# Sketched attention and a squared-ReLU MLP on one core: loads without holds, half of v on SyncE's queue, one output transfer a chunk, and a new order of work

## The chip, the core and the metric

The kernel runs on one core of a Trainium2 chip. A core has TensorE (PE, matrix products into PSUM), VectorE (DVE), ScalarE (ACT), GpSimd (POOL) and SyncE (SP), which run their own instruction streams and wait for one another through semaphores. Sixteen DMA engines move data between HBM and the core's SBUF; SyncE, ACT and GpSimd can each issue transfers, and each has its own queue on them. In the profile q1 is SyncE's queue, q10 ACT's and q0 GpSimd's. The metric is the device time of one execution in microseconds, as the median of several runs.

## The reference

q, k and v have the shape 4 batches x 4 heads x 1088 positions x 32, and S1 and S2 are 8 x 32 sketches. Each row x of q and k is mapped to 64 features, the products of the 8 numbers S1 x with the 8 numbers S2 x. Attention is then linear:

```python
q_p, k_p = (phi(q), phi(k))                 # phi: outer product of S1 x and S2 x
kv = np.einsum('bhsf,bhsd->bhfd', k_p, v)
z = np.sum(k_p, axis=2)
num = np.einsum('bhsf,bhfd->bhsd', q_p, kv)
den = np.einsum('bhsf,bhf->bhs', q_p, z)[..., None] + 1e-06
attn = num / den
x = attn.transpose(0, 2, 1, 3).reshape(B * S, H * D)      # 4352 x 128
h = x @ w_in                                # w_in 128 x 2048
r = np.maximum(h, 0.0)
out = (r * r) @ w_out                       # w_out 2048 x 128
```

## The kernel before

The four batches of attention are computed one after another, and their output columns are gathered in nine chunks for the MLP: chunks 0 and 1 come from batch 0, 2 and 3 from batch 1, and so on to 7, each of 512 tokens, and chunk 8, of 256 tokens, takes the last two positions of every group of 34 from all four batches. A chunk's MLP has 8 steps u, each over 256 of the 2048 hidden units.

The work is written as a list of small operations (ORDER, L33 to L66), and the list is emitted in that order. All of them are pinned, so each engine executes its share in the order of the list and no other. A name such as `R.1.4@A` is operation R of chunk 1, step 4, on ACT; `@V` is DVE, `@M` is one DVE instruction over two steps. The operations are:

- `kT`, `qT` (L242, L383): DVE transposes k or q of a batch. `ka` (L264): PE multiplies k with the sketches; `kc` (L284): ACT copies that out of PSUM; `kp` (L295): DVE forms the 64 features.
- `kg`, `gs`, `wz`, `wc` (L308 to L337): the sum z over the features, taken as a small product of the sketched k with itself, is multiplied with S2bd on PE (`wz`, L320) and written into the weights Wq by DVE (`wc`, L331). Wq is the right operand of `qa` (L404), so q is sketched and prepared for the denominator in one product.
- `qc` (L431) copies that out; `dt`, `dr`, `da` (L445 to L475) compute the reciprocal of the denominator and scale; `qf` and `qp` (L477, L490) form q's features and transpose them.
- `kv` (L339) multiplies k's features with v on PE, `kt`, `kr`, `kx` (L355 to L380) bring the result into the layout KV. `nd` (L508) multiplies q's features with KV, and `xe` (L537) writes the attention output as x for the MLP.
- `M` (L553) is x times w_in, `R` (L572) the ReLU, `S` (L583) the square, `O` (L593) the product with w_out, `E` (L610) copies a finished chunk to SBUF and issues its output transfers. `W` (L201) is a matmul on zeros into an idle PSUM bank.

PSUM has three pools: ps_h, two tiles of two banks for `M`; ps_o, one bank for `O`; ps_m, three banks for everything of attention. An operation that needs a tile waits until the former user of that buffer has been read.

The loads are not pinned; they are issued early, in the order of their queues. On SyncE's queue are k of batch 0, v of head 0 of batch 0, q of batch 0, and all other k and q. ACT's queue has S1 and S2 (L118, L119), v of head 1 of batch 0 (L154) and four copies of S2 into the block-diagonal S2bd (L184). GpSimd's queue has the rest of batch 0's v, w_in, w_out and v of the other batches; it also casts w_in and w_out to bf16 as they move. A k or q load moves 544 KB, one head's v 128 KB, a remainder of v (the last two positions, L139) 16 KB. The two `hold` operations (L147) copy one element on GpSimd into the k tile of batch 1 and of batch 2 out of a tile that another load fills; the load of that k tile has to come behind the copy. As the queues came out, SyncE issues k0, v0, q0, q1, q2, k3, q3, and then the held k1 and k2.

The number of semaphores for transfers is limited: eight are shared in turn by the transfers of SyncE and ACT, and eight by those of GpSimd, so an issue waits until the transfer that used its semaphore last has landed.

Of the kernel before, what the change touches and what calls it, by code (L numbers as in the profile page):

```python
# [10 lines left out]
F32 = mybir.dt.float32  # L11
# [22 lines left out]
kT.0.0 ka.0.0 kT.0.1 ka.0.1 kc.0.0 kp.0.0 kc.0.1 W.2 kg.0 gs.0 qT.0 W.1 wz.0 wc.0 W.1 qa.0.0  # L34
qc.0.0@A kv.0.0 kp.0.1 kv.0.1 kt.0 dt.0.0 dr.0.0 qa.0.1 kr.0 da.0.0 qf.0.0 qp.0.0 qc.0.1@A
dt.0.1 dr.0.1 kx.0@A W.5 nd.0.0 xe.0.0@A W.1 nd.0.1 xe.0.1@A kT.1.0 ka.1.0 kc.1.0 M.0.0 R.0.0@A
ka.1.1 kc.1.1 M.0.1 M.0.2 R.0.1@A da.0.1 R.0.2@A qf.0.1 qp.0.1 nd.1.0 xe.1.0@A kg.1 gs.1 M.0.3
qT.1 S.0.0@V S.0.1@V O.0.0 R.0.3@A M.0.4 R.0.4@A kp.1.1 wz.1 wc.1 nd.1.1 kT.2.0 M.0.5 O.0.1
M.0.6 xe.1.1@A R.0.5@A qa.1.0 S.0.4@A qa.1.1 qc.1.0@A qc.1.1@A ka.2.0 ka.2.1 kp.1.0 M.1.0
S.0.3@M O.0.2 O.0.3 R.0.6@A kc.2.1 M.1.1 kv.1.0 kv.1.1 R.1.0@A kc.2.0 kg.2 M.1.2 qT.2 R.1.1@A  # L40
kt.1 dt.1.0 gs.2 kr.1 S.0.5@A dr.1.0 M.0.7 R.1.2@A R.0.7@A S.0.6@V wz.2 kx.1@A O.0.4 O.0.5 M.1.3
R.1.3@A kT.3.0 ka.3.0 da.1.0 qf.1.0 kc.3.0 wc.2 qp.1.0 qa.2.0 qa.2.1 qf.1.1 ka.3.1 qc.2.0@A
qc.2.1@A S.0.7@V M.1.4 M.1.5 S.1.2@A kc.3.1 R.1.4@A R.1.5@A O.0.6 O.0.7 qp.1.1 nd.2.0 xe.2.0@A
M.1.6 M.1.7 kp.3.0 S.1.1@M dt.2.0 R.1.6@A kg.3 gs.3 dr.2.0 R.1.7@A nd.3.0 E.0@V da.2.0 M.2.0
xe.3.0@A M.2.1 S.1.3@V R.2.0@A O.1.0 O.1.1 S.1.5@M M.2.2 kp.2.0 O.1.2 R.2.1@A qT.3 R.2.2@A M.2.3
R.2.3@A O.1.3 O.1.4 wz.3 M.2.4 M.2.5 O.1.5 S.1.7@M R.2.4@A R.2.5@A O.1.6 O.1.7 E.1@A S.2.0@A
S.2.3@M wc.3 M.3.0 M.3.1 kp.2.1 S.2.5@M qa.4.0 qc.4.0@A R.3.0@A R.3.1@A qf.2.0 qp.2.0 qa.3.0
qa.3.1 S.2.1@A kv.2.0 kv.2.1 kt.2 M.2.6 M.2.7 R.2.6@A dt.4.0 O.2.0 O.2.1 O.2.2 O.2.3 M.3.2
qf.2.1 qp.2.1 O.2.4 R.2.7@A qc.3.0@A qc.3.1@A M.3.3 S.2.7@M kr.2 R.3.2@A R.3.3@A M.3.4 S.3.0@V
O.2.5 S.3.1@V M.3.5 O.2.6 O.2.7 R.3.4@A R.3.5@A M.3.6 M.3.7 S.3.3@M E.2@A kx.2@V nd.4.0 dt.3.0  # L50
R.3.6@A S.3.6@A xe.4.0@A kp.3.1 kv.3.0 kv.3.1 kt.3 S.3.5@M R.3.7@A nd.5.0 xe.5.0@A O.3.0 dr.3.0
da.3.0 M.4.0 M.4.1 dr.4.0 R.4.0@A qf.3.0 qf.3.1 qp.3.0 qp.3.1 O.3.1 O.3.2 R.4.1@A S.3.7@V O.3.3
M.4.2 M.4.3 R.4.2@A S.4.2@V R.4.3@A O.3.4 O.3.5 M.4.4 R.4.4@A kr.3 kx.3@V M.4.5 R.4.5@A O.3.6
O.3.7 M.5.0 M.5.1 E.3@A S.4.0@V nd.6.0 R.5.0@V S.4.1@V S.4.3@V S.5.0@V R.5.1@A M.5.2 xe.6.0@A
M.4.6 O.4.0 O.4.1 S.4.5@M R.5.2@A R.4.6@A M.4.7 R.4.7@A O.4.2 O.4.3 M.5.3 R.5.3@A M.5.4 O.4.4
R.5.4@A O.4.5 da.4.0 M.5.5 S.5.1@V qf.4.0 qp.4.0 nd.8.0 R.5.5@A S.4.7@M M.6.0 xe.8.0@A O.4.6
S.5.3@M S.5.4@V M.6.1 R.6.0@A O.4.7 M.5.6 E.4@A R.6.1@V nd.7.0 M.5.7 R.5.6@A R.5.7@A M.6.2
# [612 lines left out]
```

## Time and profile before

| | |
|---|---|
| median of 3 runs | 124.7 us (124.58 to 125.56) |
| profiled execution | 124.32 us, its span 122.5 us |
| busy PE, DVE, ACT, GpSimd | 104.1, 96.8, 86.4, 17.1 us |
| mean granted TensorE clock | 0.944 |
| moved by DMA | 10.25 MB; read 8.79 MB, written 2.23 MB |
| q1 (SyncE), q0 (GpSimd), q10 (ACT) | 6.75, 3.04, 0.20 MB |

The span begins with the first instruction and ends with the last. PE's busy share counts the time from a matmul's start to its modelled end. In the slices of the page a digit is the busy share of an engine in tenths in a 40th of the span, 3.06 us. The chain of waits follows the work that ended last back from the end, and names what each step waited for. A wait belongs to the instruction that stood at the head of its engine's queue; all that is behind it waits as well.

### The profile page before, as it was taken

To read this page: it belongs to the slowest core of one execution; us is meant where nothing else is said; L and a number is where in the kernel's file an instruction comes from. 1 tells how busy PE (TensorE), PEld (TensorE's weight loads), DVE (VectorE), ACT (ScalarE), POOL (GpSimd) and SP (SyncE) were. 2 spreads that over 40 slices of the span, in tenths; PEclk is the share of its full clock that TensorE was granted. 3 is DMA by queue.
4 is the path that set the end of the run, shared out by engine and by line. 5 is a ranking of instruction groups with operands and counts; after the bars stand their busy time and mean duration, and the time that the engine had idled before them with its cause. 6 is when DMAs were issued, how large, how long until landed. Compare 5 with 4: busy or idle time off the path is not lost.

```text
span 122.5 us, 4127 instructions
## 1 busy us (share of the span) xinstructions
PE 104.1 (85%) x1807; PEld 75.1 (61%) x1807; DVE 96.8 (79%) x153; ACT 86.4 (71%) x138; POOL 17.1 (14%) x32
## 2 busy tenths in 40 slices
PE   6094009993999999999999999999999999999950
PEld 1063007942577888756777865676666677779840
DVE  5360225938989999999999999998999799699810
ACT  4130001232789999999899999899999878979840
POOL 6600970039461000000000000000000000000000
PEclk9999655699599999999999999999999999999999
DMA  3999899968723000004013003000300300303032
GB/s 117 225 265 225 218 212 279 268 185 229 178 60 91 5 0 8 0 5 86 0 28 63 5 0 90 1 5 0 86 0 5 88 3 19 72 0 86 5 86 46
DMA packets 8633, 10.25 MB, mean 84 GB/s; under 512 B 4584, under 2 KB 6248, under 8 KB 8616
## 3 DMA queue, kind: packets, MB, share of 16 engines
q1 hardware_dynamic: 3748, 6.75, 20.3%
q0 software_dynamic: 4480, 3.04, 13.7%
q8 instruction: 14, 0.23, 0.8%
q10 hardware_dynamic: 388, 0.20, 0.7%
q14 instruction: 3, 0.02, 0.1%
HBM read 8.79 MB, written 2.23 MB: 90 GB/s over the span
## 4 chain that ended last, share of the span: by engine, by line
PE 64%; DMA 21%; ACT 8%; DVE 2%; issue 1%; DVEq 0%; SPq 0%
PE h_ps L558 24%; PE o_ps L601 22%; DMA S2bd<-in_S_dram 12%; DMA k_in<-in_k_dram 9%; PE nd_ps L528 7%; ACT r_sb L578 6%; PE kab_ps L271 3%; PE qab_ps L416 2%; PE acc_ps L346 2%; PE gg_ps L313 2%; DVE kT L248 1%; ACT g_sb L589 1%; PE kr_ps L370 1%; ACT osb L613 1%; ACT qab L433 0%
## 5 line engine op out<-in xcount | busy, mean ns | idle before, releaser
L578 ACT ACTIVATE r_sb<-h_ps 128x1024 bf16<-128x1024 f32 (+1 forms) x63 | 60.4, 1010 | 5.6 <-PE h_ps L558 5.4
L558 PE MATMUL h_ps<-xT,w_in_sb 128*128 128x512 bf16 (+1 forms) x144 | 39.2, 375 | 0.2
L601 PEld LDWEIGHTS <-g_sb 128*128 128x128 bf16 x544 | 33.4, 98 | 7.9 <-issue 0.6
L591 DVE TENSOR_TENSOR g_sb<-r_sb 128x1024 bf16<-128x1024 bf16 (+2 forms) x43 | 36.8, 885 | 1.4 <-PE o_ps L601 0.9
L601 PE MATMUL o_ps<-w_out_sb,g_sb 128*128 128x128 bf16 x544 | 36.5, 219 | 0.0
L558 PEld LDWEIGHTS <-w_in_sb 128*128 128x128 bf16 x144 | 11.8, 99 | 7.6 <-issue 3.3
L433 ACT COPY qab<-qab_ps 128x384 f32<-128x384 f32 (+1 forms) x9 | 4.1, 480 | 11.1 <-PE qab_ps L416 11.0
L300 DVE TENSOR_TENSOR kp<-kab 128x1024 f32<-128x1024 f32 (+1 forms) x8 | 10.7, 1342 | 0.9 <-ACT kab L289 0.9
L528 PE MATMUL nd_ps<-qp,KV 32*32 32x256 f32 (+2 forms) x448 | 11.2, 298 | 0.0
L495 DVE STREAM_TRANSPOSE qp<-qf 128x1024 f32<-128x1024 f32 (+1 forms) x9 | 10.5, 1178 | 0.2
L482 DVE TENSOR_TENSOR qf<-aq,qab 128x1024 f32<-128x1024 f32 (+1 forms) x9 | 10.3, 1151 | 0.1
L133 POOL DMA_DIRECT2D v_in<-in_v_dram x14 | 9.9, 710 | 3.2 <-DMA v_in<-in_v_dram 2.8
L580 DVE TENSOR_SCALAR r_sb<-h_ps 128x1024 bf16<-128x1024 f32 (+1 forms) x9 | 8.8, 984 | 1.8 <-PE h_ps L558 1.8
L388 DVE STREAM_TRANSPOSE qT<-q_in 128x512 f32<-128x512 f32 x8 | 5.2, 684 | 5.4 <-DMA q_in<-in_q_dram 5.4
L271 PE MATMUL kab_ps<-Wk,kT 128*64 128x64 f32 x136 | 6.8, 260 | 3.0 <-DVE kT L256 2.1
L589 ACT ACTIVATE g_sb<-r_sb 128x1024 bf16<-128x1024 bf16 (+1 forms) x10 | 9.1, 940 | 0.1
L528 PEld LDWEIGHTS nd_ps<-qp,KV 32*32 32x32 f32 x448 | 6.1, 105 | 4.8 <-issue 2.1
L271 PEld LDWEIGHTS kab_ps<-Wk,kT 128*64 128x64 f32 x136 | 6.1, 171 | 4.3 <-issue 2.7
L320 PE MATMUL gg_ps<-Gs,S2bd 128*128 128x32 f32 x8 | 1.6, 282 | 7.4 <-DMA S2bd<-in_S_dram 7.4
L416 PE MATMUL qab_ps<-Wq,qT 128*64 128x96 f32 x128 | 7.4, 274 | 0.0
L416 PEld LDWEIGHTS qab_ps<-Wq,qT 128*64 128x64 f32 x128 | 6.5, 157 | 1.1 <-DVE Wq L331 0.5
L248 DVE STREAM_TRANSPOSE kT<-k_in 128x1024 f32<-128x1024 f32 (+1 forms) x5 | 5.0, 1017 | 2.3 <-DMA k_in<-in_k_dram 2.3
(57 smaller groups left out, 72.8 us busy)
## 6 DMA issues: line engine op xcount, KB each, us to landing
k_in<-in_k_dram SPq DMA_DIRECT2D x4, 544.0 KB, 9.0
q_in<-in_q_dram SPq DMA_DIRECT2D x4, 544.0 KB, 12.6
out_dram<-osb SPq DMA_DIRECT2D x32, 64.0 KB, 1.6
v_in<-in_v_dram POOLq DMA_DIRECT2D x14, 128.0 KB, 7.6
w_in_sb<-in_moe_w_in_dram POOLq DMA_DIRECT2D x1, 512.0 KB, 11.9
w_out_sb<-in_moe_w_out_dram POOLq DMA_DIRECT2D x1, 512.0 KB, 13.7
v_in<-in_v_dram SPq DMA_DIRECT2D x1, 128.0 KB
v_in<-in_v_dram ACTq DMA_DIRECT2D x1, 128.0 KB
```

What stands on the lines that cost most here:

```text
L133: dma.dma_start(out=vraw[b][:, h, :NLO, :], in_=vr.rearrange("t (i l) d -> i t (l d)", i=4),)
L271: nc.tensor.matmul(kk[64 * c : 64 * c + 64, m * 64 : (m + 1) * 64], kt[:, c0 + 64 * c : c0 + 64 * c + 64], Wk.rearrange("p h x -> p (h x)" ...
L300: nc.vector.tensor_tensor(out=t[:, :n], in0=s[:, 0, :n, :, None].to_broadcast([128, n, r, r]), in1=s[:, 1, :n, None, :].to_broadcast([128, ...
L416: nc.tensor.matmul(t[64 * c : 64 * c + 64, m * H * W3 : (m + 1) * H * W3], cols, Wq[:, be].rearrange("p h x -> p (h x)"), start=True, stop ...
L482: nc.vector.tensor_tensor(out=t[:, :n], in0=T["aq", b][:, g0 : g0 + n, :, None].to_broadcast([128, n, r, r]), in1=T["qab", b][:, g0 : g0 + ...
L495: nc.vector.transpose(T["qp", b][:, :, 128 * i : 128 * i + 32 * nm].rearrange("p f (m t) -> p m f t", t=32), T["qf", b, i][:, : nm * H].re ...
L528: nc.tensor.matmul(nds[l][32 * h : 32 * h + 32, d0 : d0 + n], KV[rows, be, f, 32 * h : 32 * h + 32], src[rows, 2 * h + f, c0 : c0 + n], st ...
L558: nc.tensor.matmul(t[:, i, :N], w_in_sb[:, 2 * u + i, :], T["x", ci][:, :N], start=True, stop=True,)
L578: pin(nc.scalar.activation(t, h, ACTF.Relu))
L589: pin(nc.scalar.activation(t, s, ACTF.Square))
L591: pin(nc.vector.tensor_mul(t, s, s))
L601: nc.tensor.matmul(T["o", ci][:, m, :], T["g", ci, u // 2][:, 2 * (u % 2) + i, m * 128 : (m + 1) * 128], w_out_sb[:, ct, :], start=(ct == ...
```

## The change

It has five parts.

1. The two holds are gone. SyncE's queue gets, batch after batch, k, q and v of heads 0 and 1. GpSimd's gets v of heads 2 and 3 and the remainders of batch 0, w_in, w_out, and, at the place of `kp.0.1` in the list, the same parts of v of batches 1 to 3.
2. ACT's queue keeps S1, S2 and the four copies of S2 into S2bd.
3. The first `nd` of chunk 0's second half (`nd.0.1`) takes a tile of ps_h in place of two of ps_m.
4. For batches 1 to 3 the tokens of a chunk are laid out as before; for batch 0, `qT` splits q so that chunk 0 and chunk 1 are consecutive halves like the others. Chunk 8 orders its columns so that a partition holds two neighbouring output rows. Each chunk then leaves in one transfer of 256 KB on SyncE's queue in place of four, and chunk 8 in one on SyncE's and one on ACT's in place of two on each.
5. The whole list ORDER is a new one. Among other things `qT.0` comes ahead of `kp.0.0`, both `qa.0` are done together, `O.0.0` comes behind `M.0.7` rather than behind `M.0.3`, and `W` has 13 matmuls in all as against 14. Of the 64 full and 8 half `R`, ACT does 61 and 6 rather than 59 and 4; of the `E`, DVE does 3 rather than 1.

As the queues come out, SyncE issues k0, q0, v0 (two), k1, q1, v1 (two), k2, q2, v2, k3, q3, v3, and then nine output transfers.

```diff
-kT.0.0 ka.0.0 kT.0.1 ka.0.1 kc.0.0 kp.0.0 kc.0.1 W.2 kg.0 gs.0 qT.0 W.1 wz.0 wc.0 W.1 qa.0.0
-qc.0.0@A kv.0.0 kp.0.1 kv.0.1 kt.0 dt.0.0 dr.0.0 qa.0.1 kr.0 da.0.0 qf.0.0 qp.0.0 qc.0.1@A
-dt.0.1 dr.0.1 kx.0@A W.5 nd.0.0 xe.0.0@A W.1 nd.0.1 xe.0.1@A kT.1.0 ka.1.0 kc.1.0 M.0.0 R.0.0@A
...
+kT.0.0 kT.0.1 W.2 ka.0.0 kc.0.0 qT.0 ka.0.1 kc.0.1 W.2 kg.0 gs.0 kp.0.0 W.1 wz.0 wc.0 qa.0.0
+qa.0.1 kp.0.1 qc.0.0@A dt.0.0 dr.0.0 da.0.0 kv.0.0 qc.0.1@A qf.0.0 kv.0.1 kt.0 W.1 kr.0 kx.0@A
+qp.0.0 kT.1.0 W.3 nd.0.0 nd.0.1 xe.0.0@A xe.0.1@A ka.1.0 kc.1.0 M.0.0 R.0.0@A ka.1.1 dt.0.1
+kc.1.1 M.0.1 M.0.2 R.0.1@A kg.1 dr.0.1 da.0.1 qf.0.1 qp.0.1 gs.1 nd.1.0 wz.1 qT.1 R.0.2@A M.0.3
+wc.1 xe.1.0@A R.0.3@A S.0.0@A qa.1.0 qa.1.1 M.0.4 kp.1.0 qc.1.0@A qc.1.1@A M.0.5 R.0.4@A R.0.5@A
+kv.1.0 kp.1.1 kv.1.1 S.0.1@V kt.1 S.0.2@V nd.1.1 xe.1.1@A M.0.6 M.0.7 O.0.0 O.0.1 R.0.6@A
...
-    def hold(dst, src):
-
-        pin(nc.gpsimd.tensor_copy(dst[:1, 0, :1], src[:1, 0, :1]))
-
-    load(0, kin_t, k)
-    load_v(0, 0, nc.sync)
-    load_v(0, 1, nc.scalar)
-    load(0, qin_t, q)
-    for h in range(2, H + 2):
-        load_v(0, h, nc.gpsimd)
+    def load_v_low(b):
+        for h in range(2, H + 2):
+            load_v(b, h, nc.gpsimd)
+
+    for b in range(B):
+        load(b, kin_t, k)
+        load(b, qin_t, q)
+        for h in range(2):
+            load_v(b, h, nc.sync)
+    load_v_low(0)
...
-    hold(kin_t[1], vraw[0][:, H - 1])
-    load(1, kin_t, k)
-    load(1, qin_t, q)
...
-    for h in range(H + 2):
-        load_v(1, h, nc.gpsimd)
-    hold(kin_t[2], w_out_sb)
-    for b in (2, 3):
-        load(b, kin_t, k)
-        load(b, qin_t, q)
-    for b in (2, 3):
-        for h in range(H + 2):
-            load_v(b, h, nc.gpsimd)
...
+        if (b, gi) == (0, 1):
+            for b in range(1, B):
+                load_v_low(b)
...
+        split = "p (h l i) d -> p i h l d" if b else "p (h i l) d -> p i h l d"
...
-                    src[:, : 4 * NLO, :].rearrange("p (h l i) d -> p i h l d", h=4, i=2)[:, i],
+                    src[:, : 4 * NLO, :].rearrange(split, h=4, i=2)[:, i],
...
-                qT_rem[:, b].rearrange("p (t j) -> p j t", j=2), src[:, 4 * NLO :, :]
+                qT_rem[:, b].rearrange("p (j t) -> p j t", j=2), src[:, 4 * NLO :, :]
...
-        T["nd", ci, p] = nds = [
-            ps_m.tile([128, 512], F32, tag="m", name="nd_ps") for _ in range(2)
-        ]
+        if (ci, p) == (0, 1):
+            t = ps_h.tile([128, 2, 512], F32, tag="h", name="h_ps")
+            nds = [t[:, l] for l in range(2)]
+        else:
+            nds = [ps_m.tile([128, 512], F32, tag="m", name="nd_ps") for _ in range(2)]
+        T["nd", ci, p] = nds
...
-                dst = x[:, 128 * p : 128 * p + 128].rearrange("p (g l x) -> p g l x", g=2, l=2)
-                pin(COPY[eng](dst[:, :, l], src[:, :64].rearrange("p (g x) -> p g x", g=2)))
+                dst = x[:, 128 * l : 128 * l + 128].rearrange("p (m c t) -> p c m t", m=2, c=2)
+                pin(COPY[eng](dst[:, p], src[:, :64].rearrange("p (m t) -> p m t", m=2)))
...
-            for hi in range(4):
-                j0 = hi * NLO + (half if b == 0 else half * 4)
-                jn, step = (NLO - 1, 2) if b == 0 else (4, 1)
-                nc.sync.dma_start(
-                    out=o[:, j0 : j0 + jn : step], in_=osb[32 * hi : 32 * hi + 32, :, :]
-                )
+            o = o.rearrange("t (i l) d -> i t l d", i=4)[:, :, 4 * half : 4 * half + 4]
+            nc.sync.dma_start(
+                out=o.rearrange("i t l d -> i t (l d)"), in_=osb.rearrange("p m d -> p (m d)")
+            )
...
-            for e in range(2):
-                for g, dma in enumerate((nc.sync, nc.scalar)):
-                    dma.dma_start(
-                        out=o[2 * g + e, :, 4 * NLO :, :],
-                        in_=osb[64 * g : 64 * (g + 1), e, :],
-                    )
+            for g, dma in enumerate((nc.sync, nc.scalar)):
+                dma.dma_start(
+                    out=o[2 * g : 2 * g + 2].rearrange("b t j d -> b t (j d)"),
+                    in_=osb[64 * g : 64 * (g + 1), :2].rearrange("p m d -> p (m d)"),
+                )
```

## The prediction

> **What bounds the kernel now.** I read the page's slices first, then the chain in order of time, the waits, the timeline at the points that the chain names, and the DMA view by windows of 3 us.
>
> ```profile
> span 122.5 us, 4127 instructions
> ...
> PE   6094009993999999999999999999999999999950
> ...
> DVE  5360225938989999999999999998999799699810
> ACT  4130001232789999999899999899999878979840
> ...
> PEclk9999655699599999999999999999999999999999
> DMA  3999899968723000004013003000300300303032
> ```
>
> A slice is 3.06 us. From slice 10 (30.6 us) PE is full to the end, with ACT and DVE beside it. Before that PE has holes while the DMA engines are full: the front waits for data.
>
> ```profile
> 2.47 14.95 DMA S2bd<-in_S_dram
> ...
> 17.52 10.45 DMA k_in<-in_k_dram
> ...
> 29.46 0.69 PE kab_ps L271 x16
> ...
> 115.94 2.06 PE o_ps L601 x32
> 118.00 0.02 issue
> 118.02 0.37 ACT osb L613
> ```
>
> Two transfers carry the chain from 2.47 to 27.98 us: S2bd, four loads of 1 KB, and k of batch 1. The waits and the timeline name the place:
>
> ```profile
> PE gg_ps L320 <- DMA S2bd<-in_S_dram: 7.4, 1, 7.4
> DVE qT L388 <- DMA q_in<-in_q_dram: 5.4, 1, 5.4
> DVE kT L248 <- DMA k_in<-in_k_dram: 2.3, 1, 2.3
> ```
>
> ```profile
> 1.77 0.66 ACTq L133 DMA_DIRECT2D v_in<-in_v_dram  x1
> 2.47 0.50 ACTq L184 DMA_DIRECT2D S2bd<-in_S_dram  x1
> 18.13 0.61 PE L320 MATMUL gg_ps<-Gs,S2bd 128*128 128x32 f32 x2 [7.42 <-DMA S2bd<-in_S_dram]
> 30.08 0.68 PE L558 MATMUL h_ps<-xT,w_in_sb 128*128 128x512 bf16 x2
> ```
>
> S2bd is issued behind 128 KB of v on ACT's queue. In the DMA view of 9 to 12 us that queue (q10) moves 0.04 MB, SyncE's (q1) 0.31 and GpSimd's (q0) 0.33:
>
> ```profile
> q0 software_dynamic: 146, 0.33, 54.5%
> q1 hardware_dynamic: 83, 0.31, 34.5%
> q10 hardware_dynamic: 57, 0.04, 5.5%
> ```
>
> At some 0.013 MB a us, 0.13 MB of v takes 10 us, and S2bd lands behind it. PE waits 7.4 us for `wz` (L320); from there a serial chain (wz, qa, qc, dt to qp, nd, xe) ends in M.0.0 at 30.08, the first matmul of the second half. From M.0.0 to the end of the last `O` (118.00) are 87.9 us of full PE; 4.5 us of tail follow (E.8, two output issues a queue, landing). The execution took 124.32 us, 1.8 outside the span; the median of the runs is 124.7, so 0.4 is added at the end.
>
> ```profile
> 30.00:60.00 30.00, 30.00 (x564) 21.53 (x561) 29.17 (x43) 28.06 (x49) 4.35 (x7) 0.94 0.21 48
> 60.00:90.00 30.00, 29.85 (x522) 21.22 (x520) 29.08 (x39) 28.59 (x41) 0.00 (x0) 1.00 0.13 28
> 90.00:118.00 28.00, 27.96 (x472) 21.24 (x470) 24.50 (x33) 23.61 (x31) 0.00 (x0) 1.00 0.16 37
> ```
>
> Columns: stretch, length, busy of PE, weight loads, DVE, ACT, GpSimd, clock. Over these 88 us PE is busy 87.8, DVE 82.8, ACT 80.3: three engines near their limit. So the question is when M.0.0 starts, and whether the new order keeps the rest at 88 us.
>
> **The small loads.** Only S1, S2 and S2bd stay on ACT's queue. S1 and S2 give the price of a small load there without v: issued 0.74 and 1.37, used at 4.80. The last S2bd issue waits for a semaphore shared with k of batch 0, which is in by 5.2, where the fourth issue ends. With 4 us more S2bd is there by 9.2, and Gs, which it is multiplied with, is ready at 10.6. The 7.4 us go. Bounds: 3 us for a landing gives 8.2; the largest small-load row, 14.95, gives 17.4 (nothing gained). I take 9.2, since what stood before it in its queue is gone.
>
> The Trainium skill (DMA: Bandwidth & Descriptors, "Issuing engines are not separate DMA queues") speaks against this part: all issuing engines end on the same 16 DMA engines, and spreading issues saves only sequencer time. By that alone S2bd would land as late as before and M.0.0 would not move; the q10 row shows that the place within a queue counts.
>
> **q of batch 0** is what is late next. It landed at 14.57, issued third on SyncE's queue (k, v h0, q) beside w_in's 4 KB packets and v. Now it is second. k was in by 5.2 and v h0 only by 10.7 (the third q issue, which waits for it, ends at 11.08). q's 8 packets per DMA engine, of 4352 bytes, took 10.7 to 14.57, 0.5 us each. Started at 5.2 they end at 9.2. Bounds: 7 (no slow DMA engine) and 13.9 (14.57 less the 0.7 us issue of v h0 now behind it). I take 9.5, near the measured rate.
>
> **From q to M.0.0**, by the rows of before (DVE, in the new order): qT 1.5, kp.0.0 1.23, wc 0.19 and kp.0.1 1.48 end at 13.9; dt, dr, da with gaps 1.25; qf 1.22; qp 1.25: 17.6. Beside it PE does qa (1.5), and kv (2.15 at half clock) when v is there. The two v parts behind q on SyncE's queue have 16 packets of 1 KB per DMA engine, beside 4 KB ones some 0.3 us each: 14.5. kv then ends at 16.7; kt 0.37, kr 0.71, kx 0.37 with handovers: 18.3, so kx is last. nd.0.0 and nd.0.1 1.3, and xe.0.1 0.45: 20.1. k of batch 1 lies next on SyncE's queue, 8 packets of 0.3 to 0.5: 17 to 18.5, and kT.1.0 (1.45) and ka.1.0 (0.7), ahead of M.0.0 on PE, end by 20.6. **M.0.0 starts at 20.5** (19 to 24.9, where q lands at 13.9) instead of 30.08. Where nd.0.1 goes to the idle h buffer, its idle time before, 0.2 us in before, can go; it is within the above. The added idle matmuls lie in PE's waits: nothing, up to 0.4 each where one sits on the path. The contiguous qT_rem and x of chunk 8 keep their instruction counts: 0, between minus 0.2 and plus 0.2.
>
> **Loads behind.** No hold remains: GpSimd issues w_out at once, then v h2, h3 and the two remainders of batch 1. So w_out's 2048 packets of 256 bytes now meet a busy SyncE queue. The DMA view of 15 to 18 us, in which SyncE's queue was nearly empty, and that of 21 to 24 us show the price:
>
> ```profile
> q0 software_dynamic: 1563, 0.41, 136.9%
> q1 hardware_dynamic: 38, 0.13, 11.1%
> ...
> q1 hardware_dynamic: 159, 0.64, 80.0%
> q0 software_dynamic: 174, 0.16, 25.6%
> ```
>
> Beside a full SyncE queue GpSimd's moves packets about one for one. So w_out starts at 14.5 (w_in before it), crawls until SyncE's 5.5 MB are nearly through (2.2 MB by 14.5, then 0.25 MB a us: 27 to 28), and lands at 29; v of batch 1 behind it at 29 to 31. kv.1.0 stands on PE behind some 6.2 us of matmuls after M.0.0, paced by DVE (qp.0.1, qT.1, wc.1, kp.1.0: 5.6 us after kT.1.0, and more) to about 27.5. So PE waits 1.5 to 3.5 us in kv.1.0, with M.0.6 and all of chunk 1 queued behind it. ACT and DVE work off what they have meanwhile, and they are near the limit too: net 1.0. Bounds: 0, and all loads done as in before (v of batch 3 landed by 39; with no idle DMA slices 36): 8.5.
>
> The Trainium skill (DMA: Bandwidth & Descriptors, "SWDGE vs HWDGE vs iDMA") lets GpSimd's small descriptors travel in packets of up to 4096 bytes, and the round-robin counts packets. By that w_out would keep about half of the 0.25 MB a us and land near 20 (an estimate from this page's rule), and nothing would wait. The windows speak for one for one.
>
> **The stretch from M.0.0.** The PE work is the same: by the rows 64 M of 0.445 and 64 O of 0.446 and their halves 60.5, nd 8.8, the rest of attention 14.9: 84.2. Before took 87.9, some 1.7 of it at half clock (PEclk 5, slice 10). Counting the order: ACT gets 2 more R of 1.04 and 2 half ones of 0.60, one S more (1.07), two half S less (0.64), two E less (0.60), one kx more (0.36): plus 2.2. DVE loses four R (3.8) and S work, gains two E and the second half of dt and dr that now comes later: minus 2.5. Totals 82.5 and 80.3, still under PE. But ACT's extra lies early: up to E.2 it has 49.6 us of rows against 46.2 (times 0.92, since they overlap: 45.7 and 42.5), and PE has 41.6 and 42.7 left there: 87.3 against 85.2. I add half the difference: **88.9**; bounds 86 (no half clock) and 92 (all of it and another wait like ACT's of 60 to 71 us on the chain).
>
> **Outputs.** 24 fewer issues on SyncE, which is idle then: nothing; if that cover is wrong, 0.6 an issue. At the end one issue a queue in place of two (1.25 and 1.53): 0.65 less, tail 3.9. Bounds 0 and 0.8.
>
> **Sum:** 20.5 + 88.9 + 1.0 + 3.9 + 1.8 = 116.1, plus 0.4: **116.5**.
>
> **The rivals.**
> *Late loads (22%):* q lands at 13.9, or v of batch 1 at 36. By q: 24.9 + 88.9 + 3.9 + 2.2 = 119.9. By v: 36 plus 78.0 of PE work left plus 2 is 116, and 122.1. For it: the slow landings of before; against: queue order and full DMA.
> *All goes well (13%):* 19 + 86 + 3.9 + 2.2 = 111.1. For it: PE alone needs 84.2; against: ACT early.
> *S2bd is late anyway (6%):* it lands at 16 to 17.5, M.0.0 12 us later at 28 to 29.5 as in before: 123 to 124.5. For it: the landing of 14.95; against: the queue ahead of it is empty.
> *Slower (9%):* w_out starves behind SyncE's queue. One packet for one, at 3.3 a us per DMA engine (159 in 3 us on 16), its 128 per engine take 39 us: 53.5, if SyncE's queue stays full. v of batch 1 is behind it, so kv.1.0 starts at 54: 54 + 80 + 3.9 + 2.2 = 140. It decides from 38.6 on. Against: SyncE has 5.5 MB, not 8.
>
> **How the numbers follow.** Forecast 116.5 (114 to 119) 50%. The range 111.5 to 122 leaves out the slower case, the late S2bd and edges. A difference under 1% can hardly be told from none here; faster 0.85, same 0.06, slower 0.09.
>
> **What would show it.** S2bd gone from the chain; qT's wait ending near 9.5; M.0.0 near 20.5; a wait of acc_ps or o_ps on v or w_out near 28; PE full behind it. I am wrong if q or k of batch 1 lands later than 15 or 19, or if PE has holes after 35 us.

## The result and the profile after

The changed kernel takes 116.16 us, the median of 4 runs from 116.00 to 116.70. The kernel before, run beside it, took 125.12 (4 runs, 124.58 to 125.56). The ratio is 0.929, with a 95% interval of 0.924 to 0.935: 9.0 us faster. The forecast was 116.5. The profiled execution of the changed kernel took 116.08 us, its span is 114.3 us.

First the page's slices of the changed kernel, here 2.86 us each:

```profile
span 114.3 us, 4082 instructions
...
PE   5297679987999989999999999999999997999920
...
DVE  6185999989929999999999999999899988099700
ACT  4132315999599998799889999899999698895920
...
PEclk9999999999999999999999999999999999999995
DMA  4999999977542002000200012002101112012032
```

The slices of zeros in PE's row at 12 to 18 us are gone, and so is the half clock: the granted clock stays full until 111.3 us, which is behind the last matmul. What is left of the front is PE's 2, 7, 6 and 7 before 17 us. Behind it PE has two weaker slices, the tenth and the 34th, and the 2 and the 0 at the end.

The chain of work that ended last, in order of time (start, length, what):

```profile
4.91 1.18 POOL w_out_sb L160
6.09 0.71 POOL v_in L133
6.80 21.79 DMA v_in<-in_v_dram
28.59 0.04 issue
28.64 1.19 PE acc_ps L339 x66
```

S2bd and k of batch 1 are gone from it. The longest transfer of the chain is now a v of batch 1, issued by GpSimd at 6.80 and in by 28.59. It sits behind w_out, as the DMA issues of the page (last number: us from issue to landing) and the waits (us in total, times, longest) say:

```profile
w_out_sb<-in_moe_w_out_dram POOLq DMA_DIRECT2D x1, 512.0 KB, 22.3
```

```profile
POOL v_in L139 <- DMA w_out_sb<-in_moe_w_out_dram: 14.1, 1, 14.1
...
PEld acc_ps L339 <- DMA v_in<-in_v_dram: 3.0, 3, 1.8
...
PE acc_ps L339 <- DMA v_in<-in_v_dram: 2.4, 2, 1.6
DVE kT L236 <- DMA k_in<-in_k_dram: 2.2, 1, 2.2
```

PE waits 2.4 us in all for v: 1.64 of it in `kv.0` of batch 0, and the rest, 0.77 us, in `kv.1.0`. The view names no wait for S2bd any more, and none over 0.3 us for q. The timeline of the changed kernel (start, length, instruction, idle time before it and who ended it) gives the points that the prediction named:

```profile
7.37 1.31 DVE L382 STREAM_TRANSPOSE qT<-q_in 128x512 f32<-128x512 f32 x2 [0.30 <-DMA q_in<-in_q_dram]
...
10.89 0.38 PE L313 MATMUL gg_ps<-Gs,S2bd 128*128 128x32 f32 x2 [0.59 <-issue]
...
14.97 1.21 PE L339 MATMUL acc_ps<-kp,v_in 128*32 128x64 f32 x70 [1.64 <-DMA v_in<-in_v_dram]
...
16.75 1.25 DVE L236 STREAM_TRANSPOSE kT<-k_in 128x1024 f32<-128x1024 f32 x1
...
19.67 0.60 PE L556 MATMUL h_ps<-xT,w_in_sb 128*128 128x512 bf16 x2
...
28.27 1.56 PE L339 MATMUL acc_ps<-kp,v_in 128*32 128x64 f32 x68 [0.77 <-DMA v_in<-in_v_dram]
```

M.0.0, the first matmul of the MLP, starts at 19.67 and not at 30.08. From there PE is nearly full; the last `O` begins at 107.20 and ends at 109.25. The trace also holds a completion record, with its time, for each DMA engine that a transfer of SyncE or ACT ran on (and one at the issue, where they are fewer than 16). By these the last of the four S2bd loads was in at 10.80: PE's 0.59 us ahead of `wz`, which the view calls issue, end with it. "The stretch" is the time from M.0.0 to the end of the last `O`, "the tail" the time from there to the end of the span; the spans are given to 0.1 us. Against the steps:

| | before | predicted | after |
|---|---|---|---|
| q of batch 0 in use | 14.57 | 9.5 | 7.37 |
| S2bd in use (`wz`) | 18.13 | there by 9.2, `wz` from 10.6 | 10.89 |
| v of batch 0 all there | not the wait | 14.5 | 14.97 |
| k of batch 1 in use | 28.07 | 17 to 18.5 | 16.75 |
| M.0.0 | 30.08 | 20.5 | 19.67 |
| `kv.1.0` reached by PE | not late | 27.5 | 27.19 |
| w_out landed | 26.3 | 29 | 27.2 |
| M.0.0 to the end of the last `O` | 87.91 | 88.9 + 1.0 | 89.58 |
| tail | 4.51 | 3.9 | 5.05 |
| outside the span | 1.8 | 1.8 | 1.8 |
| profiled execution | 124.32 | 116.1 | 116.08 |

The sum is right to 0.1 us, and its terms are not: the front came 0.8 earlier, the stretch was 0.3 shorter, and the tail was 1.15 longer than the term that was set for it.

### The profile page after: what moved, and what is told of

Same layout as the page of the kernel before. It is cut to its first block, busy times and chain, and to the rows that moved or that the text cites. A ratio compares the mean times of both kernels' runs of the same rounds, so it can differ in the third digit from the quotient of the medians.

```text
span 114.3 us, 4082 instructions
## 1 busy us (share of the span) xinstructions
PE 101.0 (88%) x1806; PEld 72.2 (63%) x1806; DVE 94.3 (83%) x148; ACT 87.4 (76%) x140; POOL 12.8 (11%) x24
## 4 chain that ended last, share of the span: by engine, by line
PE 59%; DMA 19%; ACT 10%; POOL 5%; issue 3%; POOLq 0%; ACTq 0%
PE o_ps L599 23%; PE h_ps L556 22%; DMA v_in<-in_v_dram 19%; PE nd_ps L526 7%; ACT r_sb L576 6%; PE acc_ps L339 3%; PE qab_ps L411 3%; ACT g_sb L587 2%; POOL v_in L133 2%; PE gg_ps L306 1%; POOL w_out_sb L160 1%; POOL v_in L139 1%; ACT osb L611 1%; PE kr_ps L363 1%; ACT kab L277 1%
## 5 line engine op out<-in xcount | busy, mean ns | idle before, releaser
L576 ACT ACTIVATE r_sb<-h_ps 128x1024 bf16<-128x1024 f32 (+1 forms) x67 | 63.2, 999 | 5.8 <-PE h_ps L556 5.3
L599 PEld LDWEIGHTS <-g_sb 128*128 128x128 bf16 x544 | 33.7, 98 | 9.0 <-DVE g_sb L589 0.4
L599 PE MATMUL o_ps<-w_out_sb,g_sb 128*128 128x128 bf16 x544 | 37.3, 219 | 0.0
L289 DVE TENSOR_TENSOR kp<-kab 128x1024 f32<-128x1024 f32 (+1 forms) x8 | 10.6, 1337 | 0.0
L526 PE MATMUL nd_ps<-qp,KV 32*32 32x256 f32 (+2 forms) x416 | 10.1, 299 | 0.4 <-ACT r_sb L576 0.3
L477 DVE TENSOR_TENSOR qf<-aq,qab 128x1024 f32<-128x1024 f32 (+1 forms) x9 | 10.2, 1154 | 0.1
L339 PE MATMUL acc_ps<-kp,v_in 128*32 128x64 f32 x288 | 5.7, 221 | 2.5 <-DMA v_in<-in_v_dram 2.4
L339 PEld LDWEIGHTS acc_ps<-kp,v_in 128*32 128x32 f32 x288 | 4.6, 110 | 4.3 <-DMA v_in<-in_v_dram 3.0
L411 PE MATMUL qab_ps<-Wq,qT 128*64 128x96 f32 x128 | 6.2, 249 | 0.7 <-issue 0.5
L139 POOL DMA_DIRECT2D v_in<-in_v_dram x8 | 4.6, 581 | 16.8 <-DMA w_out_sb<-in_moe_w_out_dram 14.1
L411 PEld LDWEIGHTS qab_ps<-Wq,qT 128*64 128x64 f32 x128 | 5.5, 137 | 1.6 <-issue 0.6
L194 PE MATMUL idle_ps<-idle 128*128 128x512 bf16 x13 | 5.3, 508 | 1.2 <-DVE mask L166 1.2
L578 DVE TENSOR_SCALAR r_sb<-h_ps 128x1024 bf16<-128x1024 f32 (+1 forms) x5 | 5.1, 1010 | 1.1 <-PE h_ps L556 1.1
## 6 DMA issues: line engine op xcount, KB each, us to landing
w_out_sb<-in_moe_w_out_dram POOLq DMA_DIRECT2D x1, 512.0 KB, 22.3
```

What stands on the lines that cost most here:

```text
L139: dma.dma_start(out=vraw[b][32 * j2 : 32 * (j2 + 1), :, NLO, :], in_=v[b].rearrange("h (t j) d -> j t h d", j=NJ)[32 + j2],)
L289: tt.tensor_tensor(out=t[:, :n], in0=s[:, 0, :n, :, None].to_broadcast([128, n, r, r]), in1=s[:, 1, :n, None, :].to_broadcast([128, n, r, r]),
L339: nc.tensor.matmul(acc[32 * h : 32 * h + 32, :64], vraw[b][:, h, 4 * gi + m, :], t[:, m * H + h].rearrange("p i j -> p (i j)"), start=(gi ...
L411: nc.tensor.matmul(t[64 * c : 64 * c + 64, m * H * W3 : (m + 1) * H * W3], cols, Wq[:, be].rearrange("p h x -> p (h x)"), start=True, stop ...
L477: nc.vector.tensor_tensor(out=t[:, :n], in0=T["aq", b][:, g0 : g0 + n, :, None].to_broadcast([128, n, r, r]), in1=T["qab", b][:, g0 : g0 + ...
L526: nc.tensor.matmul(nds[l][32 * h : 32 * h + 32, d0 : d0 + n], KV[rows, be, f, 32 * h : 32 * h + 32], src[rows, 2 * h + f, c0 : c0 + n], st ...
```

## The experiments

Twelve kernels were run, in groups with the kernel before on the same chip; its median was 124.7 to 125.1 in each group. The theories, as they are called in the expectations: A, the loads as a whole carry the gain, since behind S2bd other loads are late too; B, S2bd's place behind v on ACT's queue alone carries it; C, the new list carries it; D, the tail grew because chunk 7's output, now one transfer, is slow and chunk 8's is queued behind it; E, `kv.1.0` waits because GpSimd's v of batch 1 stands behind w_out; F, k of batch 1 was held back by S2bd. All times are us. The first column is the median; the three that follow come from the profiled execution.

| kernel | median | M.0.0 | M.0.0 to the end of the last `O` | tail |
|---|---|---|---|---|
| before | 125.12 | 30.08 | 87.91 | 4.51 |
| after | 116.16 | 19.67 | 89.58 | 5.05 |
| before, v of head 1 from ACT's to SyncE's queue | 119.92 | 25.91 | 87.59 | 4.60 |
| before, S2bd ahead of v on ACT's queue | 122.00 | 29.02 | 86.41 | 4.57 |
| before, no holds | 123.12 | 29.66 | 86.49 | 4.55 |
| before, all the new loads | 118.27 | 23.96 | 87.54 | 4.30 |
| after, all the old loads | 125.85 | 30.48 | 88.29 | 5.43 |
| after, v of head 1 back on ACT's queue | 121.71 | 27.46 | 87.31 | 5.13 |
| after, `nd.0.1` in ps_m | 117.39 | 20.34 | 89.24 | 5.12 |
| after, GpSimd's v of batch 1 ahead of w_out | 117.39 | 22.23 | 87.93 | 5.04 |
| after, all v of batch 1 on SyncE, chunk 7 in four | 119.24 | 21.47 | 92.61 | 3.72 |
| after, chunk 7's output in four | 115.49 | 19.97 | 89.46 | 3.97 |
| the last, and v of batch 1 ahead of w_out | 116.72 | 22.95 | 87.46 | 3.99 |
| after, every chunk's output in four | 115.18 | 20.18 | 89.39 | 3.73 |

### Before, with v of head 1 off ACT's queue

```diff
     load_v(0, 0, nc.sync)
-    load_v(0, 1, nc.scalar)
     load(0, qin_t, q)
+    load_v(0, 1, nc.sync)
```

> The kernel before, with one load moved: v of head 1 of batch 0 goes from ACT's queue to SyncE's, behind q of batch 0. Theory A (the front is a row of late loads, and taking one away uncovers the next): S2bd lands by 9 us, but q of batch 0 still lands at 14 to 15 us and k of batch 1, issued at about 17.5 us, at 28 us, and ka.1.0 stands before M.0.0 on PE; M.0.0 at 29 to 30 us, 123 to 125.5 us. Theory B (S2bd alone carried the front): M.0.0 moves by the 7.4 us that PE waited for it, to about 23 us, and the time is 117 to 119 us.

The four runs lie far apart, 117.39 to 125.76, with the granted clock between 0.957 and 0.994 (the fastest run had the highest), so the median of 119.92 can't decide between the theories; the profiled one took 119.84 at a clock of 0.968. Its timeline is the better witness for the order of events: `wz` runs at 10.74 and waits for no load, `qT.0` starts at 11.10 after a wait of 2.14, M.0.0 at 25.91. So moving 128 KB off ACT's queue does free S2bd, as both theories had it. What theory A had next on the path, k of batch 1 staying late by its hold, did not come about: it was issued at 12.01 rather than 17.52 and was used at 23.61, and it is still the last wait ahead of M.0.0, 3.49 us. That left a question: why was it issued late in the kernel before?

### Before, with S2bd ahead of v on ACT's queue

```diff
-    load_v(0, 1, nc.scalar)
     load(0, qin_t, q)
...
         nc.scalar.dma_start(out=S2bd[r * h : r * h + r, h, :], in_=S2)
+    load_v(0, 1, nc.scalar)
```

> The kernel before, with the four loads of S2bd issued on ACT's queue ahead of v of head 1 instead of behind it; nothing moves to another queue and the holds stay. Theory F (k of batch 1 was issued late because its issue shares a semaphore with a load of S2bd, so S2bd delayed both): S2bd by 11 us, k of batch 1 issued at 12 to 15 us and landed at 23 to 26 us, M.0.0 at 25 to 28 us, 119 to 122.5 us. If S2bd and k of batch 1 are late for separate reasons: k lands near 28 us as before, M.0.0 at 29 to 30 us, 123.5 to 125 us.

Median 122.0, ratio to before 0.974 (0.967 to 0.981). The timeline of this kernel, SyncE's queue and TensorE:

```profile
11.40 0.60 PE L320 MATMUL gg_ps<-Gs,S2bd 128*128 128x32 f32 x2 [0.66 <-issue]
...
13.68 13.15 SPq L145 DMA_DIRECT2D k_in<-in_k_dram  x2
...
20.82 2.14 PE L346 MATMUL acc_ps<-kp,v_in 128*32 128x64 f32 x70 [4.59 <-DMA v_in<-in_v_dram]
```

The last S2bd load is in at 11.30 and `wz` runs at 11.40. k of batch 1 is issued at 13.68, with its hold in place (GpSimd's copy for it ran at 11.58). In before that copy ran at 12.43, and the issue came at 17.52. So in before the hold was over, and something else kept k back. SyncE's own waits and its issues in before say what:

```profile
SPq L145 <- DMA v_in<-in_v_dram: 9.9, 2, 7.7
```

```profile
14.56 0.33 SPq L145 DMA_DIRECT2D k_in<-in_k_dram  x1
17.08 0.33 SPq L145 DMA_DIRECT2D q_in<-in_q_dram  x1
17.52 9.35 SPq L145 DMA_DIRECT2D k_in<-in_k_dram  x2
```

The issue at 17.08 is q of batch 3, which stands ahead of k of batch 1. It needs the semaphore that v of head 1 had on ACT's queue, and that load's last record is at 17.06: 2.2 us of waiting, the second of the two waits in the first line. k of batch 1 itself needs the semaphore of the first S2bd load, in at 17.42, and goes out 0.10 us later, so S2bd comes last and is what the chain shows. Theory F is right that shared semaphores held k back, and incomplete: v of head 1 and S2bd, both late on ACT's queue, each held SyncE. This edit frees SyncE from both. Here v lands as late as 20.77, but its semaphore is needed by no early issue on SyncE's queue, and k goes out 0.94 us behind the landing of q of batch 0 (12.74). That landing came 1.8 us earlier than in before, so about 2 of the 3.8 us by which k's issue moved are the semaphores'.

The gain is only 3 us all the same, and 1.5 of it lies behind M.0.0: v of head 1 is now last on ACT's queue, PE waits 4.59 us for it in `kv.0`, and M.0.0 comes at 29.02. The change's answer is to leave only six small loads on that queue.

### Before, without the holds

```diff
-    hold(kin_t[1], vraw[0][:, H - 1])
...
-    hold(kin_t[2], w_out_sb)
```

> The kernel before without the two holds; all else stays, v of head 1 ahead of S2bd on ACT's queue too. k of batch 1 is issued fourth and lands by 20 us. S2bd still lands near 17 us, so wz starts near 18 us and M.0.0 near 28 us: 121.5 to 124 us. If the holds were the main cause: below 120 us.

Median 123.12, ratio 0.987 (0.980 to 0.994). SyncE now issues k of batch 1 at 2.46, and yet:

```profile
20.15 0.60 PE L318 MATMUL gg_ps<-Gs,S2bd 128*128 128x32 f32 x2 [9.62 <-DMA S2bd<-in_S_dram]
```

With more in flight on the other queues S2bd lands 2 us later still, and M.0.0 starts at 29.66. The ratio makes it 1.6 us faster. In the profiles 1.4 of it lies in the stretch behind M.0.0, where the granted clock is full here, and half from 30.5 to 33.9 us in before. So the holds' own worth isn't settled: the run of before with the fullest clock in this group, 0.999, took 123.17, and this kernel took 122.54 at 1.00.

### Before, with all the new loads

The edit is the first half of the code diff shown with the change (the loads on the three queues and their place), and leaves the list ORDER, the outputs and PSUM as they were.

> The kernel before with the changed kernel's loads (queues, order, no holds) and nothing else of the change: the old list ORDER, four output transfers a chunk, the old layouts. Theory A (the loads make the gain): q lands near 7.4 us as in the changed kernel, M.0.0 at 20 to 22 us, then 86 to 88 us and the old tail of 4.5 us: 114 to 118 us. Rival C (the new order of work makes the gain): above 121 us.

Median 118.27 (117.87 to 118.64): the loads alone make 6.5 of the 8.6 to 9 us. M.0.0 starts at 23.96 in the old list, and `wz` (11.99) waits for no load. Theory C is out as the main cause.

### After, with the old loads

The inverse of that edit, in the changed kernel.

> The changed kernel with the loads of the kernel before, holds and all; order of work, outputs and layouts stay new. Theory A: S2bd lands near 17 us and k of batch 1 near 28 us again, M.0.0 at 29 to 30 us, 124 to 127 us. Rival C: 116 to 119 us. w_out has little beside it from 15 to 18 us, as in the kernel before, so there is no wait in kv.1.0.

Median 125.85 (125.16 to 126.04). S2bd is waited for again, 9.06 us until 18.98, and M.0.0 starts at 30.48. The new list, the PSUM tile and the outputs bring nothing where the loads are late. The two together: the new list is worth 4.3 us at the front (23.96 to 19.67), but only when the data is there. Of these 2.1 are left in the median (118.27 to 116.16), for the stretch is 2.0 longer with it and the tail 0.75.

### After, with v of head 1 back on ACT's queue

```diff
-            load_v(b, h, nc.sync)
+            load_v(b, h, nc.scalar if (b, h) == (0, 1) else nc.sync)
```

> The changed kernel with v of head 1 of batch 0 back on ACT's queue, ahead of S2bd. Theory A (place within a queue counts): S2bd lands behind that v at 14 to 17 us in place of before 10.9 us, wz and with it qa wait 4 to 6 us, M.0.0 near 24 us, 119 to 122 us. The skill's rule that all queues share the same 16 DMA engines, taken alone, gives no change: 116 us.

Median 121.71 (120.62 to 122.95): one load of 128 KB, put on the queue ahead of S2bd, takes back 5.5 of the 9 us.

```profile
18.16 0.61 PE L313 MATMUL gg_ps<-Gs,S2bd 128*128 128x32 f32 x2 [7.14 <-DMA S2bd<-in_S_dram]
```

PE waits 7.14 us, as it did in before (7.42). This is the direct test of the place in the queue. By the Trainium skill (DMA: Bandwidth & Descriptors, "Issuing engines are not separate DMA queues"), taken alone, which grants separate issuers only the sequencer's time, this edit should have left the 116 us alone. The bytes are the same in both kernels; what differs is the queue that this v stands on.

The completion records show how the place in the queue acts. This v has records from 4 DMA engines, at 15.44 to 16.39. The first S2bd load has 8: four at 8.57 to 8.94, and four at 15.99 to 16.86, each 0.5 to 0.7 us after one of v's. In before it is the same (v 15.37 to 17.06; S2bd four at 5.75 to 6.38 and four at 15.71 to 17.42). So half of S2bd's rows came early even behind v, and it was the half that shares four DMA engines with v that PE waited for.

### After, with `nd.0.1` in the pool of attention

```diff
-        if (ci, p) == (0, 1):
+        if False:
```

> The changed kernel, with nd.0.1 in the attention's PSUM pool as before. nd.0.1 needs two buffers of three of which nd.0.0 holds two, so its second half waits for xe.0.0: M.0.0 0.3 to 1.0 us later, 116.4 to 117.2 us. If the prediction's 0.2 us or less is right: 116.1 to 116.4 us.

Median 117.39, but its six runs go from 116.44 to 119.15, and the profiled one took 116.45. In that, M.0.0 starts 0.67 later than in after. `kT.0.0` starts 0.53 later too (6.17, behind S1 and S2, which came later), but that is made up by the end of `kv.0`, 0.09 later. From the end of `kv.0` to M.0.0 it is 4.07 against 3.49 us. So the idle tile may be worth some 0.6 us on the way to M.0.0; 0.2 was predicted. At the span's end it is 0.4. The runs don't settle it closer.

### After, with v of batch 1 ahead of w_out

```diff
     nc.gpsimd.dma_start(out=w_in_sb, in_=moe_w_in.rearrange("d (ct c) -> d ct c", c=128))
+    load_v_low(1)
     w_out_sb = consts.tile([128, C_TILES, 128], BF16)
...
-            for b in range(1, B):
+            for b in range(2, B):
```

> The changed kernel, with GpSimd's part of v of batch 1 issued ahead of w_out. Theory E (kv.1.0 waits for that v because it stands behind w_out): the wait of acc_ps near 27 us goes, w_out lands 1 to 2 us later, near 28.5 us, still ahead of O.0.0 at 31 us; 114.7 to 115.7 us. Rival (ACT sets the pace there, the wait is beside it): no change, 116.0 to 116.4 us. Rival (w_out becomes the wait): o_ps waits, 116.5 us or more.

A miss: 117.39 (116.99 to 117.83), 1.2 slower than after. What it was made for did work: the 0.77 us in `kv.1.0` are gone, and the stretch from M.0.0 is 1.65 us shorter (87.93). But v of batch 0 became late:

```profile
16.04 1.21 PE L340 MATMUL acc_ps<-kp,v_in 128*32 128x64 f32 x70 [2.67 <-DMA v_in<-in_v_dram]
```

It waits until 16.04 in place of 14.97, and M.0.0 starts at 22.23, 2.6 later. So 1.1 us of that is the later v, a load on SyncE's queue, though only GpSimd's order was changed. The page's DMA row has 8 or 9 in every slice from 3 to 29 us, so the likely reason is that the 288 KB that go earlier push others back; no run shows it apart. The other 1.5 lie between `kv.0` and M.0.0. There the granted clock is 0.81 and 0.64, where the changed kernel had 1.00 (stretch, length, busy of PE, weight loads, DVE, ACT, GpSimd, clock, share and GB/s of the DMA); this kernel first, then the changed one:

```profile
16.00:19.00 3.00, 2.48 (x75) 2.15 (x77) 2.12 (x3) 0.49 (x2) 2.06 (x4) 0.81 1.40 279
19.00:22.20 3.20, 3.20 (x83) 1.94 (x81) 3.03 (x7) 1.13 (x5) 0.48 (x1) 0.64 1.29 273
```

```profile
15.00:19.67 4.67, 4.51 (x158) 3.29 (x159) 4.50 (x9) 1.61 (x6) 0.00 (x0) 1.00 1.21 261
```

The clock fell here behind PE's wait for v. The three matmuls of `W` ahead of `nd.0.0` take 1.49 us rather than 0.81, and `nd.0.0` starts at 20.06, 0.8 us after the copy of KV has ended: this is one place where the half clock sits on the serial chain. Whether it would have stayed full with the shorter wait can't be told from this run.

### After, with all of v of batch 1 on SyncE's queue

```diff
-        for h in range(2):
+        for h in range(H + 2 if b == 1 else 2):
             load_v(b, h, nc.sync)
...
-            for b in range(1, B):
+            for b in range(2, B):
```

Chunk 7's output is in four transfers here as well, as below.

> The changed kernel with chunk 7 in four transfers and all of v of batch 1 on SyncE's queue, ahead of k of batch 2, so that none of it stands behind w_out and batch 0's loads keep their company. Theory E (the wait in kv.1.0 is the place behind w_out, and the loss of the last try came from what v took from batch 0's loads): M.0.0 stays at 19.5 to 20.5 us, no wait of acc_ps near 27 us, the stretch to the last O 87.5 to 88.5 us; 113.5 to 114.8 us. Rival (ACT or k of batches 2 and 3, now 0.3 MB later, set the pace): 115 us or more.

A larger miss: 119.24 (118.77 to 119.60). Two loads now stand ahead of what is needed:

```profile
28.54 0.56 SPq L145 DMA_DIRECT2D k_in<-in_k_dram  x1
...
31.96 1.19 PE L339 MATMUL acc_ps<-kp,v_in 128*32 128x64 f32 x66 [3.09 <-DMA v_in<-in_v_dram]
...
39.23 1.25 DVE L236 STREAM_TRANSPOSE kT<-k_in 128x1024 f32<-128x1024 f32 x1 [4.69 <-DMA k_in<-in_k_dram]
```

PE waits 3.09 us in `kv.1.0` rather than 0.77, and DVE 4.69 for k of batch 3, which SyncE issues at 28.54. The stretch grows to 92.61, and from 33.7 to 37.1 us of it the clock is at half. On SyncE's queue each of the two head loads of v has completion records from 4 DMA engines. The wait for v that is left in the changed kernel was not to be had for nothing in either of the two ways tried.

### After, with chunk 7's output in four transfers

```diff
-            nc.sync.dma_start(
-                out=o.rearrange("i t l d -> i t (l d)"), in_=osb.rearrange("p m d -> p (m d)")
-            )
+            for i in range(4) if ci == 7 else ():
+                nc.sync.dma_start(
+                    out=o[i].rearrange("t l d -> t (l d)"),
+                    in_=osb[32 * i : 32 * i + 32].rearrange("p m d -> p (m d)"),
+                )
+            if ci < 7:
+                nc.sync.dma_start(
+                    out=o.rearrange("i t l d -> i t (l d)"), in_=osb.rearrange("p m d -> p (m d)")
+                )
```

> The changed kernel, but chunk 7 leaves in four transfers of 64 KB, one for each group of 32 partitions, in place of one of 256 KB. Theory D (the single transfer is worked off by 4 DMA engines, over 4.5 us, and chunk 8's rows on SyncE's queue end behind it): the time from the end of the last O to the end of the span falls from 5.05 to 4.3 to 4.5 us, 115.4 to 115.7 us. Rival (one issue less a queue makes the tail shorter, as the prediction had it): four issues cost 0 to 1.2 us more, 116.2 to 117.4 us.

Median 115.49 (six runs, 114.77 to 118.58; ratio to before 0.937, 0.929 to 0.946), the profiled one 115.21. The medians alone don't tell it from the changed kernel; the tail does, 3.97 in place of 5.05. The DMA view of the last stretch shows why. A digit is the busy share of the 16 engines in a 40th of the window; first the changed kernel from 107 to 114.3, then this one from 107 to 113.4:

```profile
DMA  0000000127025011213126546876322100000000
...
q1 hardware_dynamic: 212, 0.33, 19.5%
...
out_dram<-osb SPq DMA_DIRECT2D x1, 256.0 KB
```

```profile
DMA  0000000492492581592000000599910000000000
...
q1 hardware_dynamic: 272, 0.33, 21.5%
...
out_dram<-osb SPq DMA_DIRECT2D x5, 64.0 KB
```

Both move 0.33 MB on SyncE's queue. Each of the four transfers of 64 KB is a peak of 9, 9, 8 and 9 tenths, and they are over at 110.0, just behind the issue of chunk 8's rows (109.86). The one transfer of 256 KB, issued at 107.17, runs at 0 to 3 tenths for most of its time, and its four records are at 112.5 to 113.0. Chunk 8's rows are issued in the middle of it, at 109.69, on SyncE's queue and on ACT's. On both, 12 of their 16 records are in by 112.6, and the last four come at 112.65 to 113.16 on SyncE's and 112.83 to 113.33 on ACT's; with chunk 7 in four all are in by 112.11. So theory D holds but for the word "queued": the transfer of chunk 8 that ended last stood on ACT's queue, where nothing was ahead of it. What the two queues have in common is the DMA engines.

The number of engines is in the completion records: the transfer of 256 KB has them from 4 DMA engines, each small one from 16. The Trainium skill (DMA: Bandwidth & Descriptors, "Why a DMA increments its semaphore by 16 and not by 1") has a rule that gives these counts: the number of engines is the largest one up to 16 that divides the slowest dimension of both sides, and on the DRAM side that dimension is 4 for the whole chunk and 32 for a quarter.

### Chunk 7 in four, and v of batch 1 ahead of w_out

The edits of the kernel above and of the one with v of batch 1 ahead of w_out, together.

> Both: chunk 7 in four transfers and v of batch 1 ahead of w_out. If theories D and E hold and the gains add: 114.2 to 115.2 us.

A miss for the reason already seen: M.0.0 at 22.95, stretch 87.46, tail 3.99, median 116.72 (116.14 to 117.34). The two edits add up, and one of them costs more than it brings.

### After, with every chunk's output in four transfers

```diff
-            nc.sync.dma_start(
-                out=o.rearrange("i t l d -> i t (l d)"), in_=osb.rearrange("p m d -> p (m d)")
-            )
+            for i in range(4):
+                nc.sync.dma_start(
+                    out=o[i].rearrange("t l d -> t (l d)"),
+                    in_=osb[32 * i : 32 * i + 32].rearrange("p m d -> p (m d)"),
+                )
```

> The changed kernel with four transfers of 64 KB for every chunk, not only chunk 7. If only the last chunk's transfer is on the path: as with chunk 7 alone, 115.0 to 115.7 us, the time from the last O to the end of the span near 4.0 us. If 24 more issues on SyncE cost anything: above 115.8 us.

Median 115.18 (114.62 to 116.03), ratio 0.922 (0.916 to 0.928): the fastest median of all. Its profiled span, 113.3, is 1.0 below that of the changed kernel, where the tail is 1.3 shorter (3.73). The intervals of the ratios, this one and the changed kernel's, overlap, so the gain over the changed kernel rests on the tail in the two profiles, not on the medians alone. Against the kernel above, in which only the last chunk is split, nothing is lost: 21 more issues on SyncE cost nothing that can be seen, and it is the last chunk that counts. So "one transfer a chunk" is the part of the change that the runs show to do harm. With chunk 8's single issue a queue, and chunk 7 in four, the tail is 3.73 to 3.97, against 4.30 to 4.60 in the kernels with the old outputs; no run tried that single issue by itself.

## Why the prediction was right, and where it was not

**S2bd and its place.** Right. Putting v back on ACT's queue costs 5.5 us, and `wz` waits 7.14 us again. My 9.2 for the landing was early, though: three of the four loads were in by 8.9, and the fourth, issued only at 5.47, by 10.80, 0.09 us ahead of `wz`. In the two kernels that differ from the changed one in their output transfers alone, PE's idle time of 1.2 and 1.4 us ahead of `wz` (at 11.53 and 11.08) is ended by S2bd. So S2bd has nothing to spare. The early 9.2 did little harm, since I had set `wz` at 10.6 for Gs. The gain of 9 us is mostly that of the loads: 6.5 in the old list.

**What was late in the kernel before.** Read wrong in one point, without harm to the number. I followed the chain from S2bd to k of batch 1 as two transfers one behind the other and took the second as due to the hold and the queue. SyncE's waits said more: the issues ahead of k and of k itself waited for semaphores that v of head 1 and S2bd had on ACT's queue. With v of head 1 moved away from ahead of S2bd, k was issued at 12.0 and 13.7 with the holds in place. I priced k of batch 1 by its new place in the queue instead, 17 to 18.5; it was in use at 16.75.

**q and the way to M.0.0.** q was there at 7.37, not 9.5, near my lower bound of 7. The step that failed is "0.5 us each" for its packets: by the completion records of before, q's packets did not run one after another from 10.7 to 14.57; 15 of its 16 DMA engines were done between 6.3 and 11.0, and one at 14.55. In the new place all 16 were done between 5.3 and 7.3. It bought little, for `wz` had to wait for S2bd until 10.80 (Gs was ready at 10.2): `wz` 10.89, `qa` 11.55. The last wait of the front was v of batch 0 at 14.97. I had 14.5, by luck in part: I spread its two parts over all DMA engines, "16 packets of 1 KB per DMA engine", and the records have each on 4 engines, in by 11.74 and 14.93. Then came `kx` and `nd` as worked out. M.0.0 came 0.8 earlier than 20.5, inside the bounds.

**w_out and v of batch 1.** Right in the wait, and lucky in the number. w_out took 22.3 us to land against 13.7, and PE reached `kv.1.0` at 27.19 and waited. In the DMA view of 18 to 21 us GpSimd's queue moved 329 packets and 0.26 MB beside 198 and 0.37 MB on SyncE's, as "packet for packet" would have it. But it was not an even crawl: by 19.04, near the 20 that I had weighed and left, 1805 of w_out's 2048 packets were through and 12 of its 16 completion records in; the other 243 packets took until 26.5, at most four at a time, and the last four records came at 25.7 to 27.2. Nor was SyncE's queue nearly through at 27 to 28, as I had it: 4.6 of its 5.5 MB had moved by 27, and its last load landed at 38.9. The step that failed is to price the queues as if every transfer lay evenly on the 16 DMA engines. k of batch 1 shows the same split: 12 records by 12.0, and four at 15.7 to 16.7, behind v's last at 14.9.

**The stretch.** 89.58 against 88.9 + 1.0, right by luck, for the shares were wrong. The runs let it be taken apart. The old list without half clock behind M.0.0 needs 86.4 to 86.5 (before with S2bd first, and without holds), so 1.4 to 1.5 of before's 87.91 was the half clock, which lasted 3.4 us there; with 2.6 and 2.7 us of it (all the new loads, and v of head 1 off ACT's queue) the old list needs 87.5 and 87.6. The new list at full clock and with v of batch 1 in time needs 87.3 (v of head 1 back on ACT's queue, where w_out landed at 21.4): 0.9 more than the old, near the 1.0 that I charged for ACT's early work, though no run shows that ACT's share is its cause. The wait for v then costs 1.65 to 2.3 (89.58 less 87.93 or 87.31), more than my 1.0 and more than the 0.77 us that PE waits in `kv.1.0`; where the rest of it lies was not traced. I had left the half clock in, since I could not tell whether it would go, and had undersized the wait. The two made up for each other.

**The outputs.** Wrong. The step that failed is "at the end one issue a queue in place of two: 0.65 less, tail 3.9". The tail was 5.05. The issue part is true, as the runs with chunk 7 in four show (3.73 to 3.97). What I priced at nothing, "24 fewer issues on SyncE", is where the loss sat: I counted issues and bytes, and not how many DMA engines a transfer of this shape runs on. Chunk 7's one transfer on 4 DMA engines is still under way when chunk 8's are issued, and four of the 16 pieces of each of these come last. It costs 1.1 to 1.3 us.

**The rivals.** None came about. q came at 7.4 and v of batch 1 at 28.6, not at 13.9 or 36; S2bd was not late; w_out was in at 27.2, not at 53.5.

## What to carry to other kernels

In a front that waits for data, read each queue as a line of people: ask of every load what is ahead of it, and put the small load that gates a serial chain alone, or first, on its queue; then look at which issue waits for a semaphore of a transfer that has nothing to do with it. Count on how many DMA engines a transfer has completion records: one on a few engines holds up its share of what comes behind it. Once the DMA engines are full, a load that goes earlier can make another one late, on other queues too, so price a reordering by the load that becomes late. Merging output transfers saves issues that may be free and can take engines away from the transfer: look at the last one of the kernel, where nothing hides it.

## What the runs showed of the hardware that was not expected

- A store of 256 KB whose outer dimension is 4 on the DRAM side ran on 4 DMA engines, from its issue at 107.17 to near 113; four stores of 64 KB on 16 engines, issued from 107.35 on, were through at 110.0. It made 1.1 us of the tail.
- The load of one head's v, 128 KB, whose outer dimension on the DRAM side is 4 too, ran on 4 DMA engines on SyncE's and ACT's queues. Of what came behind it on its queue, part was early and four pieces were late: the first S2bd load in before (four of 8 by 6.4, four by 17.4), k of batch 1 in the changed kernel (12 of 16 by 12.0, four by 16.7). What a v spread over 16 engines would bring was not tried.
- Issues on one engine can be held by a transfer of another engine. In before q of batch 3 on SyncE's queue was issued at 17.08, on the landing of v of head 1 from ACT's queue (17.06), and k of batch 1 behind it at 17.52, on that of S2bd (17.42); k went out at 12.0 and 13.7 where neither held SyncE.
- The granted clock was full until 111.3 us, behind the last matmul, in the changed kernel's profile, and half from 13.4 to 23.7 and from 30.5 to 33.9 us in before. In all four profiles in which `wz` waits 7 us and more for S2bd it is half for 10.2 us on end, from 12.3 to 14.2 us on; in the others it came for 3.4 or 6.8 us at a time or not at all, and not by the length of the wait alone (none with a wait of 4.59 us, S2bd first on ACT's queue; 3.4 us with one of 2.67). What decides it was not tested. Where most of it lies inside a wait it cost nothing that can be seen: without the holds, one run took 122.49 us at a mean clock of 0.95 and one 122.54 at 1.00.
- With 4 loads put ahead of w_out on GpSimd's queue, v of batch 0 on SyncE's queue came 1.1 us later, with the order and the bytes of SyncE's queue unchanged.
